# Another emission order for a fused linear-attention and gated feed-forward kernel

## The chip, the cores and the metric

The kernel runs on one core of one Trainium2 chip. The metric is the device time of one execution in microseconds (us), the median of several runs. The core has five engines with a queue each, which take their own instructions strictly in the order in which the program emitted them: TensorE (PE in the profile, its weight loads PEld), VectorE (DVE), ScalarE (ACT), GpSimd (POOL) and SyncE (SP, which here only issues transfers). Sixteen DMA engines move data between the chip's memory and the on-chip memory; they are fed by the queue of SP (q1 in the profile) and that of POOL (q0).

## The reference

```python
# attention, for each batch b of 4, head h of 8, step t of 768; head size 48
cur = einsum('bhd,bhe->bhde', u * k_t, v_t)
y_t = einsum('bhd,bhde->bhe', r_t, state + cur)
state = w_t[..., None] * state + einsum('bhd,bhe->bhde', k_t, v_t)
# feed-forward on x = y as (3072 tokens, 384)
xn  = x / sqrt(mean(x * x) + 1e-6) * rms_g
g   = xn @ w_gate                      # 384 x 1536
out = (g * sigmoid(g) * (xn @ w_val)) @ w_out
```

Inputs and output are float32; the kernel's matrix products run in bf16.

## The kernel before, in words

The 768 steps are cut into six **stages** n = 0 to 5 of 128 steps; each stage holds the four batches j = 0 to 3, so 512 tokens. Work is written as small named steps `name.n.j`; in the feed-forward steps the third number f = 0 to 11 is a block of 128 of the 1536 hidden units. One text, `ORDER` (line 25 on), lists all 1106 steps; the loop at the end of the kernel calls them one by one, and each call emits its instructions. So the order on every engine, in the load queue of SP and in the queue of POOL is written out by hand: a step that waits holds up all later steps of its engine. `ORDER` also sets which PSUM bank a step gets: `psum` takes, from a ring of two banks ("a" and "b") or four ("q"), a free one whose last use is oldest, so a matrix product may also have to wait for the last reader of what was in its bank.

One stage and batch of the attention, in the order of its data, with the lines of the profile in brackets:

- `load_r`, `load_k`, `load_v` (L244): 192 KB each on SP's queue. `load_w` (L257): 384 KB for stages 0 and 1 together, later 192 KB.
- `ln`, then `cs_mm` on PE (L391 to L409), the running sum of logarithms; `exp_r`, `exp_k` on ACT (L231); from stage 2 on `cs_add` on DVE (L417) between them.
- `r_mul` on DVE (L440), `k_mul` on DVE in stage 0 and on POOL later (L446), `w_tot` (L436).
- `rk_pe` on PE (L469) and `rk_tr` on ACT (L478) transpose the two in stages 0 and 1; from stage 2 on `rk_tr` is a transposing transfer on SP (L474).
- `q_mm` (L487, L489) multiplies them, and `q_mask_e` (DVE, L494), `q_copy_o` (ACT, L498) and `q_mask_o` (POOL, L505; in stage 0 DVE, L502) mask the result.
- `cast_v` (ACT, L374, in stages 0 and 1; POOL, L376, later), `st_mm` (L515) and `st_new` (DVE, L521 and L522) carry the state from stage to stage.
- `bonus_mul` (two POOL instructions, L452 and L453), `bonus_sum` (DVE, L457) and `bonus_v` (POOL, L462) make the term with u.
- `y_mm` (L535), `x_add` (DVE, L540); `x_sq` (ACT, L545), `x_rstd` (ACT in stage 0, POOL later, L553 and L554), `xn_mul` (ACT, L558); `xn_pe` (L569) and `xn_out` (DVE, L580) transpose the normalized rows into `xnt` in stages 0 to 3; in stages 4 and 5 `xn_tr` and `xn_gain` do so with transfers.

The feed-forward of a stage needs `xnt` of all four batches: `gate_mm` and `val_mm` (both L598, three matrix products 128x512 each), `silu` on ACT (L231) and `h_mul` on DVE (L616), for twelve f, then `o_mm` (L630, twelve products), `o_out` and `out_dma` (L645) for four batches. `gate_mm` uses ring "a", `val_mm` ring "b". While PE does the feed-forward of stage n, the attention of stage n + 1 is worked in between, and `o_mm` of a stage fills the time at the next boundary between stages.

Weights come over POOL's own DMA queue: `load_gv` (L346) brings w_gate (tile `wg_sb`) and w_val (tile `wv_sb`). `load_gv.0.1` and `load_gv.0.0` are w_val and w_gate for f = 0 to 3 (384 KB each in bf16), `load_gv.1.0` and `load_gv.1.1` are w_gate and w_val for f = 4 to 11 (768 KB each). `load_wo` brings w_out in three parts. They stand in POOL's queue, so each is issued when POOL reaches it.

Finally 48 steps `warm` (L369) are single matrix products on zeros; nobody reads them, and they keep PE at work while it has nothing else to do.

What holds the buffers: eight each of `rt`, `kt`, `vt`, three of `ruk`, six of `ydiag` and `rkT`.

Of the kernel before, what the change touches and what calls it, by code (L numbers as in the profile page):

```python
# [55 lines left out]
xn_mul.1.0 bonus_v.1.3 x_add.1.3 cs_mm.2.0 cs_add.2.0 st_new.1.2 x_sq.1.3 o_mm.0.0 o_out.0.0 out_dma.0.0 load_v.2.2
exp_r.2.0 w_tot.2.0 r_mul.2.0 w_tot.2.1 r_mul.2.1 o_mm.0.1 xn_pe.1.0 load_k.2.3 xn_out.1.0 exp_k.2.1 ln.2.2 cs_mm.2.2
cs_add.2.2 x_rstd.1.1 x_rstd.1.2 st_mm.1.3 st_new.1.3 xn_mul.1.2 xn_pe.1.2 xn_out.1.2 ln.2.3 cs_mm.2.3 o_mm.0.2
x_rstd.1.3 o_out.0.1 xn_mul.1.3 xn_pe.1.3 exp_k.2.0 xn_mul.1.1 xn_pe.1.1 exp_r.2.2 bonus_mul.2.1 k_mul.2.1 load_k.2.2
rk_tr.2.1 k_mul.2.0 rk_tr.2.0 bonus_mul.2.0 cast_v.2.1 o_mm.0.3 cs_add.2.3 exp_k.2.3 k_mul.2.3 xn_out.1.1 xn_out.1.3  # L60
load_v.2.0 w_tot.2.2 load_v.3.2 load_v.3.0 load_v.2.3 r_mul.2.2 bonus_mul.2.3 cast_v.2.2 exp_k.2.2 k_mul.2.2 rk_tr.2.2
exp_r.2.3 r_mul.2.3 rk_tr.2.3 load_w.3.0 load_k.3.1 w_tot.2.3 cast_v.2.0 o_out.0.2 gate_mm.1.7 silu.1.7 bonus_sum.2.1
bonus_v.2.1 bonus_sum.2.0 gate_mm.1.1 silu.1.1 val_mm.1.1 h_mul.1.1 val_mm.1.0 gate_mm.1.6 silu.1.6 val_mm.1.6
h_mul.1.6 load_r.3.1 out_dma.0.1 load_w.3.2 load_w.3.1 st_mm.2.1 st_new.2.1 gate_mm.1.0 gate_mm.1.5 silu.1.0 h_mul.1.0
load_r.3.2 o_out.0.3 out_dma.0.3 load_k.3.0 silu.1.5 val_mm.1.5 h_mul.1.5 gate_mm.1.4 silu.1.4 q_mm.2.0 q_mask_e.2.1
q_copy_o.2.0 q_mask_o.2.0 bonus_sum.2.3 q_mask_e.2.0 q_copy_o.2.1 q_mask_o.2.1 val_mm.1.7 h_mul.1.7 gate_mm.1.8
silu.1.8 st_mm.2.0 st_mm.2.2 gate_mm.1.9 st_new.2.2 load_w.3.3 bonus_v.2.0 bonus_v.2.3 bonus_mul.2.2 st_new.2.0
y_mm.2.1 gate_mm.1.3 silu.1.3 val_mm.1.3 h_mul.1.3 y_mm.2.0 gate_mm.1.2 load_r.3.0 load_r.3.3 x_add.2.0 val_mm.1.2
silu.1.2 h_mul.1.2 x_sq.2.0 silu.1.9 cast_v.2.3 cast_v.3.0 x_rstd.2.0 val_mm.1.4 h_mul.1.4 gate_mm.1.10 silu.1.10
x_add.2.1 x_sq.2.1 load_k.3.2 val_mm.1.9 h_mul.1.9 q_mm.2.2 q_mask_e.2.3 q_copy_o.2.2 load_k.3.3 out_dma.0.2  # L70
# [612 lines left out]
```

## Time and profile before

| what | value |
|---|---|
| runs shown | 203.05, 203.21 and 203.41 us, median 203.21 us |
| profiled execution, first to last instruction (span) | 202.2 us |
| median of the runs less that span | 1.0 us |
| instructions | 4444 |
| mean granted TensorE clock | 0.999 |
| busy: DVE, ACT, POOL | 146.1, 136.6, 134.3 us |
| bytes read from the chip's memory, written | 25.96 MB, 4.72 MB |
| first product of the feed-forward (`val_mm.0.2`) | 33.19 us after the span's start |
| last product of the kernel (`o_mm.5.4`) ends | 199.3 us |

The page lists each engine's busy time, the span in 40 slices of about 5.06 us with a busy digit in tenths for each, the DMA queues, the chain of work that ended last, and groups of instructions by line. Busy time of PE is modelled, since matrix products are pipelined: two that follow each other overlap in the list by about 0.2 us, so starts are compared here rather than ends. A time such as "33.19" is counted from the start of the span. The execution's own time is known as its span; what lies around it is taken as the 1.0 us of the table.

### The profile page before, as it was taken

What the parts mean: (1) busy time and instruction counts of PE and PEld (TensorE: products, weight loads), DVE (VectorE), ACT (ScalarE), POOL (GpSimd) and SP (SyncE); (2) the same over time, 40 slices, a digit from 0 to 9 for tenths busy, and PEclk for the clock granted to TensorE, in tenths of its full rate; (3) what the DMA queues carried; (4) which work ended last, traced back from release to release, by engine and by line L of the source; (5) the groups of instructions that cost most, each with busy time, mean ns of one, the idle gap of its engine ahead of it and who ended that gap; (6) DMA issues with size and microseconds to landing.
All of it is one profiled execution on the core that took longest, in us unless ns stands there. A gap on an engine that the chain in (4) does not pass through costs nothing.

```text
span 202.2 us, 4444 instructions
## 1 busy us (share of the span) xinstructions
PE 192.6 (95%) x1600; PEld 113.5 (56%) x1600; DVE 146.1 (72%) x289; ACT 136.6 (68%) x278; POOL 134.3 (66%) x198
## 2 busy tenths in 40 slices
PE   1999988899999999999999999999999999999994
...
GB/s 152 243 244 177 209 182 202 202 161 201 199 192 221 196 179 238 225 133 194 177 231 245 206 171 195 216 241 134 24 192 112 15 68 71 45 3 117 0 97 99
DMA packets 121566, 32.41 MB, mean 160 GB/s; under 512 B 116420, under 2 KB 120392, under 8 KB 121544
## 3 DMA queue, kind: packets, MB, share of 16 engines
...
HBM read 25.96 MB, written 4.72 MB: 152 GB/s over the span
## 4 chain that ended last, share of the span: by engine, by line
PE 79%; SPq 8%; DMA 8%; POOL 2%; issue 1%; ACT 0%; POOLq 0%
PE ps_av L598 12%; PE ps_bu L598 12%; PE ps_bv L598 10%; PE ps_au L598 10%; PE ps_qx L630 8%; PE ps_qv L630 7%; SPq L244 7%; DMA wg_sb<-in_moe_w_gate_dram 6%; PE ps_qz L630 5%; PE ps_qu L630 3%; SPq L257 2%; DMA kt<-in_k_dram 2%; PE ps_qu L487 1%; PE ps_av L406 1%; PE ps_qu L515 1%
## 5 line engine op out<-in xcount | busy, mean ns | idle before, releaser
L630 PEld LDWEIGHTS <-ht 128*128 128x128 bf16 x300 | 28.3, 98 | 16.9
L231 ACT ACTIVATE sg<-ps_av 128x512 bf16<-128x512 f32 x38 | 22.7, 598 | 18.4 <-PE ps_av L598 16.8
L616 DVE TENSOR_TENSOR ht<-ps_bu,sg 128x512 bf16<-128x512 f32 x38 | 26.1, 686 | 11.7 <-PE ps_bu L598 8.4
L598 PEld LDWEIGHTS <-wg_sb 128*128 128x128 bf16 x216 | 22.8, 114 | 20.2 <-DMA wg_sb<-in_moe_w_gate_dram 2.1
L598 PEld LDWEIGHTS <-wv_sb 128*128 128x128 bf16 x216 | 23.2, 114 | 19.3 <-DVE xnt L580 0.2
L616 DVE TENSOR_TENSOR ht<-ps_bv,sg 128x512 bf16<-128x512 f32 x34 | 23.3, 686 | 12.2 <-PE ps_bv L598 8.8
L452 POOL TENSOR_TENSOR ruk<-rt,kt 128x384 f32<-128x384 f32 x24 | 24.0, 1000 | 11.1 <-DMA kt<-in_k_dram 6.0
L598 PE MATMUL ps_av<-xnt,wg_sb 128*128 128x512 bf16 x114 | 30.9, 380 | 0.4 <-DMA wg_sb<-in_moe_w_gate_dram 0.4
L231 ACT ACTIVATE sg<-ps_au 128x512 bf16<-128x512 f32 x34 | 20.4, 599 | 16.0 <-PE ps_au L598 14.6
L598 PE MATMUL ps_bu<-xnt,wv_sb 128*128 128x512 bf16 x114 | 30.9, 380 | 0.0
L598 PE MATMUL ps_au<-xnt,wg_sb 128*128 128x512 bf16 x102 | 27.7, 381 | 0.8 <-DMA wg_sb<-in_moe_w_gate_dram 0.8
L598 PE MATMUL ps_bv<-xnt,wv_sb 128*128 128x512 bf16 x102 | 27.7, 380 | 0.0
L453 POOL TENSOR_TENSOR ruk<-ruk,u_bc 128x384 f32<-128x384 f32 x24 | 23.9, 997 | 1.9
L462 POOL TENSOR_TENSOR ydiag<-vt,diag 128x384 f32<-128x384 f32 x24 | 19.7, 830 | 0.9 <-DVE diag L457 0.8
L446 POOL TENSOR_TENSOR rk<-kt,ek 128x384 bf16<-128x384 f32 x20 | 19.9, 1003 | 0.3 <-ACT ek L231 0.3
L505 POOL TENSOR_SCALAR_AFFINE_SELECT qts<-qts 128x512 bf16<-128x512 bf16 x20 | 12.5, 636 | 10.7 <-ACT qts L498 10.7
L630 PE MATMUL ps_qx<-wo_sb,ht 128*128 128x384 bf16 x96 | 16.9, 326 | 0.0
L630 PE MATMUL ps_qv<-wo_sb,ht 128*128 128x384 bf16 (+1 forms) x96 | 15.9, 316 | 0.0
L558 ACT ACTIVATE xn<-xb,rstd 128x384 bf16<-128x384 f32 x24 | 14.1, 608 | 1.2 <-POOL rstd L554 1.2
L457 DVE TENSOR_REDUCE diag<-ruk 128x8 f32<-128x384 f32 x24 | 12.9, 543 | 2.7 <-POOL ruk L453 2.7
L231 ACT ACTIVATE lw<-wt 128x384 bf16<-128x384 f32 (+1 forms) x20 | 11.2, 579 | 4.6 <-DMA wt<-in_w_dram 4.5
L229 ACT ACT_TABLE_LOAD x10 | 12.8, 1283 | 1.8 <-PEq L667 1.6
...
## 6 DMA issues: line engine op xcount, KB each, us to landing
...
wg_sb<-in_moe_w_gate_dram POOLq DMA_DIRECT2D x1, 768.0 KB, 12.0
```

Of the source, the lines that this page charges most:

```text
L229: nc.scalar.preload_act_table_set(table_name)
L231: return nc.scalar.activation(**kw).ins
L244: dmas["load_" + which, n, j] = nc.sync.dma_start(out=inp[which, n, j], in_=t[j, :, n * L:(n + 1) * L, :].rearrange("h t d -> t h d")).ins
L446: eng.tensor_tensor(out=rk[:, n % 2, j, 1, :, 0:D], in0=inp["k", n, j], in1=bank["cs_k", n, j][:, 0:DM].rearrange("p (h d) -> p h d", h=H) ...
L452: nc.gpsimd.tensor_tensor(out=ruk[n, j], in0=inp["r", n, j], in1=inp["k", n, j], op=ALU.mult)
L453: nc.gpsimd.tensor_tensor(out=ruk[n, j], in0=ruk[n, j], in1=u_bc, op=ALU.mult)
L457: nc.vector.tensor_reduce(out=diag[n, j].rearrange("p h o -> p (h o)"), in_=ruk[n, j], axis=mybir.AxisListType.X, op=ALU.add)
L462: nc.gpsimd.tensor_tensor(out=ydiag[n, j], in0=inp["v", n, j], in1=diag[n, j].to_broadcast([128, H, D]), op=ALU.mult)
L558: nc.scalar.activation(out=xn, in_=xb[n, j], func=AF.Copy, scale=rstd[n, j][:, 1:2])
L598: nc.tensor.matmul(ps, lhsT=units(ws, c, f), rhs=xnt[n][:, c, :], start=(c == 0), stop=(c == KC - 1))
L616: nc.vector.tensor_tensor(out=ht[n][:, f, :], in0=bank.pop(("v", n, f)), in1=bank.pop(("sg", n, f)), op=ALU.mult)
L630: nc.tensor.matmul(ps[:, cols], lhsT=ht[n][:, f, b * L:(b + 1) * L], rhs=wo_sb[:, f, cols], start=(f == 0), stop=(f == FC - 1))
```

## The change

The list of steps is the same, step for step; its order is another one on every engine, in SP's load queue and in POOL's queue. With the order the choice of PSUM banks changes too, by the rule above. Two constants are written in another way: `EXPK_SB` still holds the same pairs, since `K_POOL` has 10 to 13 as well, and `GV_BEHIND` has a third `None`, which nothing reads.

What can be seen when the order is read engine by engine: on PE, 43 of the 48 `warm` steps stand ahead of the first `cs_mm`, and all 48 ahead of the first `rk_pe` (before: 5 ahead of the first `cs_mm`, and the rest spread up to the start of the feed-forward). In SP's queue the first twenty loads are in another order. In POOL's queue `load_gv.0.1`, `load_gv.0.0` and `load_gv.1.0` follow each other with nothing between them, and `load_gv.1.1` comes six steps of attention later. From stage 1 on most steps of the attention stand somewhat earlier among the products of the feed-forward. The start of the list, and the lines further down that the prediction speaks of:

```diff
-load_r.0.1 load_w.0.1 load_k.0.0 load_k.0.1 ln.0.1 warm.31.0 load_w.0.0 ln.0.0 warm.0.0 warm.13.0 warm.28.0
-bonus_mul.0.1 bonus_sum.0.1 load_r.0.0 load_v.0.0 bonus_mul.0.0 load_w.0.2 load_w.0.3 warm.29.0 load_k.0.2 load_v.0.1
-load_r.0.2 bonus_mul.0.2 load_r.0.3 load_v.0.3 load_v.0.2 bonus_v.0.1 load_r.1.3 load_k.1.0 cs_mm.0.1 exp_k.0.1
-warm.10.0 warm.17.0 warm.33.0 warm.38.0 exp_r.0.1 r_mul.0.1 k_mul.0.1 bonus_sum.0.0 bonus_v.0.0 cs_mm.0.0 exp_r.0.0
-ln.0.2 exp_k.0.0 cast_v.0.0 r_mul.0.0 k_mul.0.0 w_tot.0.0 warm.8.0 warm.16.0 warm.12.0 warm.4.0 warm.30.0 w_tot.0.1
-rk_pe.0.1 warm.15.0 warm.14.0 load_k.0.3 bonus_mul.0.3 load_r.1.1 load_r.1.0 load_k.1.1 load_v.1.1 load_r.1.2 ln.0.3
-load_k.1.3 warm.20.0 warm.37.0 warm.2.0 warm.22.0 warm.23.0 warm.5.0 warm.3.0 rk_pe.0.0 warm.24.0 load_gv.0.1
-load_k.1.2 load_v.1.0 load_w.2.1 warm.25.0 load_v.1.2 load_w.2.0 load_v.1.3 load_r.2.1 load_r.2.0 load_w.2.2 warm.32.0
-warm.27.0 st_mm.0.0 st_new.0.0 load_w.2.3 cs_mm.0.2 rk_tr.0.1 q_mm.0.1 warm.19.0 rk_tr.0.0 exp_r.0.2 cast_v.0.1
-r_mul.0.2 warm.7.0 cs_mm.0.3 q_mask_e.0.1 q_mm.0.0 warm.6.0 warm.18.0 warm.11.0 warm.26.0 warm.1.0 warm.21.0 warm.36.0
-exp_k.0.2 w_tot.0.2 k_mul.0.2 rk_pe.0.2 q_mask_e.0.0 bonus_sum.0.2 bonus_v.0.2 exp_r.0.3 w_tot.0.3 q_mask_o.0.0
-r_mul.0.3 warm.39.0 y_mm.0.0 warm.9.0 cs_mm.1.0 cast_v.0.3 q_mask_o.0.1 x_add.0.0 load_k.2.1 load_gv.0.0 cast_v.0.2
-exp_k.0.3 k_mul.0.3 rk_tr.0.2 q_mm.0.2 q_mask_o.0.2 q_mask_e.0.2 y_mm.0.1 x_add.0.1 exp_r.1.0 bonus_sum.0.3 r_mul.1.0
-rk_pe.0.3 cs_mm.1.1 x_sq.0.0 warm.34.0 x_rstd.0.0 rk_tr.0.3 q_mm.0.3 q_mask_o.0.3 exp_r.1.1 exp_k.1.0 exp_k.1.1
-warm.40.0 warm.35.0 x_sq.0.1 x_rstd.0.1 xn_mul.0.0 xn_mul.0.1 y_mm.0.2 q_mask_e.0.3 warm.44.0 warm.42.0 x_add.0.2
-warm.41.0 st_mm.0.3 st_new.0.3 warm.43.0 x_sq.0.2 x_rstd.0.2 w_tot.1.1 w_tot.1.0 bonus_v.0.3 y_mm.0.3 x_add.0.3
-x_sq.0.3 xn_mul.0.2 x_rstd.0.3 xn_pe.0.0 xn_out.0.0 st_mm.0.2 xn_pe.0.1 cs_mm.1.3 exp_r.1.3 st_new.0.2 xn_out.0.1
-r_mul.1.1 load_gv.1.0 k_mul.1.0 st_mm.0.1 warm.47.0 rk_pe.1.0 warm.45.0 st_new.0.1 xn_pe.0.2 xn_out.0.2 cs_mm.1.2
-xn_mul.0.3 exp_k.1.3 xn_pe.0.3 r_mul.1.3 xn_out.0.3 cast_v.1.1 k_mul.1.1 load_gv.1.1 rk_pe.1.1 st_mm.1.1 exp_k.1.2
-exp_r.1.2 w_tot.1.2 r_mul.1.2 w_tot.1.3 bonus_mul.1.3 val_mm.0.2 val_mm.0.3 warm.46.0 gate_mm.0.2 gate_mm.0.3 rk_tr.1.1
-q_mm.1.1 silu.0.2 h_mul.0.2 load_k.2.0 silu.0.3 h_mul.0.3 bonus_sum.1.3 st_new.1.1 gate_mm.0.0 val_mm.0.1 rk_tr.1.0
-bonus_mul.1.0 val_mm.0.0 load_r.2.3 silu.0.0 q_mask_e.1.1 h_mul.0.0 bonus_mul.1.1 bonus_sum.1.1 gate_mm.0.6 silu.0.6
-gate_mm.0.1 silu.0.1 q_mm.1.0 q_copy_o.1.0 gate_mm.0.5 silu.0.5 h_mul.0.1 q_mask_e.1.0 bonus_sum.1.0 gate_mm.0.7
-silu.0.7 load_r.2.2 k_mul.1.3 rk_pe.1.3 q_mask_o.1.0 gate_mm.0.9 k_mul.1.2 rk_pe.1.2 q_copy_o.1.1 rk_tr.1.2 gate_mm.0.4
-cast_v.1.0 load_wo.0.0 val_mm.0.6 h_mul.0.6 val_mm.0.5 h_mul.0.5 y_mm.1.0 bonus_v.1.1 bonus_v.1.0 x_add.1.0 load_v.2.1
-st_mm.1.0 st_new.1.0 rk_tr.1.3 silu.0.9 val_mm.0.4 val_mm.0.7 silu.0.4 h_mul.0.4 h_mul.0.7 x_sq.1.0 cast_v.1.2
...
+load_k.0.0 load_r.0.0 load_w.0.0 load_v.0.1 load_w.0.2 load_w.0.1 load_v.0.0 bonus_mul.0.0 warm.24.0 load_r.0.1
+warm.10.0 warm.22.0 warm.29.0 warm.17.0 warm.4.0 warm.43.0 warm.26.0 ln.0.1 cast_v.0.1 ln.0.2 ln.0.0 cast_v.0.0
+warm.39.0 warm.31.0 warm.19.0 load_w.0.3 warm.18.0 load_k.0.1 bonus_sum.0.0 bonus_v.0.0 bonus_mul.0.1 warm.32.0
+warm.16.0 bonus_sum.0.1 warm.33.0 warm.14.0 warm.40.0 warm.42.0 warm.8.0 warm.5.0 warm.27.0 load_k.0.2 warm.28.0
+warm.2.0 warm.11.0 warm.3.0 warm.30.0 warm.37.0 load_r.0.2 load_v.1.1 bonus_mul.0.2 warm.23.0 warm.41.0 load_k.0.3
+warm.1.0 warm.34.0 warm.36.0 warm.20.0 warm.7.0 load_k.1.0 load_r.0.3 warm.0.0 warm.35.0 warm.13.0 warm.25.0 warm.9.0
+ln.0.3 warm.38.0 warm.12.0 warm.6.0 warm.15.0 cs_mm.0.1 exp_r.0.1 warm.21.0 warm.45.0 cs_mm.0.0 r_mul.0.1 exp_k.0.1
+k_mul.0.1 warm.47.0 warm.46.0 warm.44.0 load_r.1.1 load_v.0.3 w_tot.0.1 exp_k.0.0 exp_r.0.0 rk_pe.0.1 load_v.0.2
+k_mul.0.0 rk_tr.0.1 r_mul.0.0 st_mm.0.0 w_tot.0.0 st_new.0.0 rk_pe.0.0 rk_tr.0.0 bonus_sum.0.2 q_mm.0.1 q_mask_e.0.1
+q_mask_o.0.1 cs_mm.0.2 cast_v.1.1 bonus_mul.0.3 bonus_v.0.1 exp_k.0.2 exp_r.0.2 q_mm.0.0 q_mask_e.0.0 k_mul.0.2
+cs_mm.0.3 cast_v.0.3 r_mul.0.2 y_mm.0.1 q_mask_o.0.0 rk_pe.0.2 exp_k.0.3 y_mm.0.0 k_mul.0.3 cast_v.0.2 exp_r.0.3
+w_tot.0.2 rk_tr.0.2 x_add.0.0 bonus_v.0.2 load_gv.0.1 st_mm.0.3 load_r.1.0 load_k.1.1 load_k.1.2 w_tot.0.3 r_mul.0.3
+cs_mm.1.0 load_gv.0.0 load_gv.1.0 bonus_mul.1.0 q_mm.0.2 load_r.1.3 load_r.1.2 load_k.1.3 x_add.0.1 cs_mm.1.1
+q_mask_o.0.2 q_mask_e.0.2 x_sq.0.0 x_rstd.0.0 st_new.0.3 rk_pe.0.3 exp_k.1.0 xn_mul.0.0 st_mm.0.1 y_mm.0.2 exp_r.1.1
+rk_tr.0.3 xn_pe.0.0 load_v.1.0 w_tot.1.1 x_add.0.2 r_mul.1.1 load_v.1.2 load_v.1.3 bonus_sum.0.3 q_mm.0.3 exp_k.1.1
+x_sq.0.1 cs_mm.1.3 q_mask_e.0.3 q_mask_o.0.3 exp_r.1.0 k_mul.1.1 bonus_v.0.3 k_mul.1.0 rk_pe.1.1 y_mm.0.3 x_rstd.0.1
+x_sq.0.2 xn_out.0.0 w_tot.1.0 x_add.0.3 r_mul.1.0 xn_mul.0.1 st_mm.0.2 load_w.2.1 load_w.2.0 x_rstd.0.2 st_mm.1.1
+x_sq.0.3 xn_mul.0.2 x_rstd.0.3 xn_mul.0.3 cs_mm.1.2 st_new.0.1 st_new.0.2 xn_pe.0.2 xn_pe.0.1 xn_out.0.2 xn_out.0.1
+exp_r.1.3 bonus_mul.1.3 xn_pe.0.3 rk_pe.1.0 exp_k.1.3 k_mul.1.3 load_gv.1.1 exp_k.1.2 xn_out.0.3 bonus_sum.1.0
+bonus_mul.1.1 rk_tr.1.1 exp_r.1.2 val_mm.0.3 r_mul.1.3 w_tot.1.3 w_tot.1.2 r_mul.1.2 val_mm.0.2 q_mm.1.1 gate_mm.0.2
+gate_mm.0.3 silu.0.2 bonus_v.1.0 load_w.2.3 load_w.2.2 load_r.2.1 k_mul.1.2 q_mask_e.1.1 silu.0.3 st_new.1.1 rk_pe.1.3
+gate_mm.0.0 h_mul.0.3 h_mul.0.2 bonus_sum.1.1 rk_tr.1.0 gate_mm.0.1 q_mm.1.0 q_copy_o.1.1 cast_v.1.0 val_mm.0.1
+st_mm.1.0 val_mm.0.0 silu.0.0 silu.0.1 q_copy_o.1.0 gate_mm.0.6 q_mask_o.1.0 h_mul.0.0 q_mask_e.1.0 h_mul.0.1 silu.0.6
+rk_pe.1.2 gate_mm.0.5 st_new.1.0 gate_mm.0.7 silu.0.5 bonus_v.1.1 load_wo.2.0 load_r.2.0 y_mm.1.0 silu.0.7 rk_tr.1.3
+gate_mm.0.9 gate_mm.0.4 x_add.1.0 load_wo.0.0 bonus_mul.1.2 bonus_sum.1.3 val_mm.0.6 q_mm.1.3 h_mul.0.6 bonus_sum.1.2
+rk_tr.1.2 val_mm.0.5 q_mm.1.2 x_sq.1.0 cast_v.1.2 q_copy_o.1.3 val_mm.0.4 h_mul.0.5 q_mask_e.1.2 st_mm.1.2 val_mm.0.7
+x_rstd.1.0 q_mask_o.1.1 bonus_v.1.3 silu.0.4 load_wo.1.0 silu.0.9 h_mul.0.4 q_mask_e.1.3 h_mul.0.7 q_mask_o.1.3
...
+x_add.1.2 st_mm.1.3 val_mm.0.8 val_mm.0.10 x_add.1.3 x_add.1.1 xn_out.1.0 load_k.2.1 h_mul.0.8 ln.2.0 cs_mm.2.1
...
+o_mm.0.3 w_tot.2.2 k_mul.2.0 rk_tr.2.0 r_mul.2.3 w_tot.2.3 load_v.2.0 r_mul.2.2 st_new.2.1 bonus_mul.2.0 gate_mm.1.7
+val_mm.1.1 load_k.2.2 silu.1.7 k_mul.2.3 bonus_mul.2.3 cast_v.2.0 load_v.2.2 gate_mm.1.1 val_mm.1.0 gate_mm.1.6
+k_mul.2.2 silu.1.1 silu.1.6 o_out.0.3 gate_mm.1.0 h_mul.1.1 bonus_sum.2.0 bonus_sum.2.1 silu.1.0 cast_v.2.2 val_mm.1.6
...
+q_mask_o.2.0 q_mask_o.2.1 load_r.3.1 load_k.3.1 st_mm.2.0 gate_mm.1.4 st_mm.2.2 h_mul.1.5 rk_tr.2.3 load_v.2.3
...
+q_mask_o.3.2 q_copy_o.3.3 load_w.4.0 q_mask_o.3.3 x_add.3.1 silu.2.8 h_mul.2.3 y_mm.3.2 st_mm.3.3 bonus_v.3.2 x_sq.3.1
+x_rstd.3.1 load_r.4.1 load_w.4.2 load_r.4.3 x_add.3.2 silu.2.9 y_mm.3.3 x_sq.3.2 x_rstd.3.2 cast_v.4.0 xn_pe.3.0
...
+bonus_mul.4.1 bonus_mul.4.3 o_mm.2.1 cs_mm.4.0 load_v.4.2 out_dma.1.3 st_new.3.3 cs_add.4.0 exp_r.4.0 ln.4.2 cs_mm.4.1
...
+load_w.5.1 o_mm.2.2 cs_mm.4.2 load_v.5.1 out_dma.2.1 w_tot.4.1 r_mul.4.1 xn_out.3.3 cs_add.4.2 k_mul.4.0 k_mul.4.1
+o_mm.2.0 cs_mm.4.3 st_mm.4.0 o_out.2.2 exp_r.4.2 xn_out.3.1 cs_add.4.3 r_mul.4.2 bonus_sum.4.3 exp_k.4.3 exp_r.4.3
...
+x_sq.4.2 xn_tr.4.3 load_k.5.1 cs_mm.5.0 xn_tr.4.1 bonus_mul.5.3 cs_add.5.0 cs_mm.5.1 cs_add.5.1 exp_r.5.0 o_mm.3.1
+xn_gain.4.0 x_rstd.4.2 r_mul.5.0 cs_mm.5.3 exp_k.5.0 exp_r.5.1 xn_mul.4.2 bonus_sum.5.3 o_mm.3.2 st_new.4.2 k_mul.5.0
...
-    EXPK_SB = sel("10 11 12 13") | K_POOL
+    EXPK_SB = sel("") | K_POOL
...
-    GV_BEHIND = (None, None)
+    GV_BEHIND = (None, None, None)
```

142 lines of the change are left out of this document (65 added, 77 removed).

## The prediction, as it was put on record

> **What bounds the kernel now.** I read the page first: busy times, slices, chain.
>
> ```profile
> PE 192.6 (95%) x1600; PEld 113.5 (56%) x1600; DVE 146.1 (72%) x289; ACT 136.6 (68%) x278; POOL 134.3 (66%) x198
> ...
> PE   1999988899999999999999999999999999999994
> ...
> PE 79%; SPq 8%; DMA 8%; POOL 2%; issue 1%; ACT 0%; POOLq 0%
> ```
>
> PE is the bound, and the chain is PE from about 40 us on. Next the table of windows, for the rest of the run:
>
> ```profile
> 45.00:199.30 154.30, 154.29 (x1239) 91.25 (x1237) 116.72 (x222) 104.78 (x215) 105.42 (x155) 1.00 0.71 150
> ```
>
> PE (second number) fills 154.29 of 154.30 us. An order can win nothing there but the few tenths at which products start late. The waits of PE, and its timeline around the handoff to the feed-forward:
>
> ```profile
> PE ps_qu L328 <- POOL ones_row L324: 4.1, 1, 4.1
> PE ps_au L598 <- DMA wg_sb<-in_moe_w_gate_dram: 0.8, 1, 0.8
> PE ps_qu L535 <- DVE qts L502: 0.6, 1, 0.6
> PE ps_av L598 <- DMA wg_sb<-in_moe_w_gate_dram: 0.4, 1, 0.4
> ```
>
> ```profile
> 33.19 0.81 PE L598 MATMUL ps_bu<-xnt,wv_sb 128*128 128x512 bf16 x3
> ...
> 34.48 0.33 PE L369 MATMUL ps_qz<-zero 128*128 128x384 bf16 x1
> 35.64 0.84 PE L598 MATMUL ps_au<-xnt,wg_sb 128*128 128x512 bf16 x3 [0.83 <-DMA wg_sb<-in_moe_w_gate_dram]
> ...
> 39.90 0.84 PE L598 MATMUL ps_av<-xnt,wg_sb 128*128 128x512 bf16 x3 [0.38 <-DMA wg_sb<-in_moe_w_gate_dram]
> ```
>
> So two val_mm start at 33.19, but the first gate_mm waits for w_gate until 35.64, and gate_mm.0.6 for its second part until 39.90. Where those transfers come from, in POOL's timeline (L346 issues them):
>
> ```profile
> 22.47 1.00 POOL L452 TENSOR_TENSOR ruk<-rt,kt 128x384 f32<-128x384 f32 x1 [3.39 <-DMA kt<-in_k_dram]
> ...
> 24.49 0.99 POOL L346 DMA_DIRECT2D wv_sb<-in_moe_w_val_dram  x1
> ...
> 26.29 0.81 POOL L346 DMA_DIRECT2D wg_sb<-in_moe_w_gate_dram  x1
> ...
> 27.90 0.80 POOL L346 DMA_DIRECT2D wg_sb<-in_moe_w_gate_dram  x1
> ```
>
> They stand behind the last bonus_mul of stage 0, which waits for k(0,3). Time is decided by **when the feed-forward starts and what PE loses after that**.
>
> **The yardstick.** PE's work left after a step is the sum of starts to starts: 0.648 us a gate_mm or val_mm, 1.948 an o_mm, 0.553 a paired q_mm, 0.446 an rk_pe, 0.374 a y_mm, 0.17 an st_mm or xn_pe, 0.27 a cs_mm. After gate_mm.0.2 that is 161.3 us in the old order, 161.0 in the new one (q_mm.1.1 is done by then). Start plus work left: before, 35.64 + 161.3 = 196.9; the last product ended at 199.3, so 2.4 us were lost later: 0.55 at gate_mm.0.6, 0.15 at val_mm.1.8, 1.7 in tenths at changes of shape, which I carry over.
>
> **The start, walked through.** Loads: the first 22 landings of before, by bytes ahead of them, give the clock of SP's queue (4,224 KB at 22.40, 4,416 KB at 23.20). In the new order r(0,3) is item 16 (3,840 KB, 20.4), v(0,3) 18 (22.4), v(0,2) 19 (23.2); before, k(0,3) was last at 22.4.
>
> Warm products: PE starts them at 5.94 as before, 0.32 each until the clock rises at about 11.1 (16 of them), then 0.163: 43 end at 15.5. Only then comes cs_mm.0.1, 8 us later than before (7.51). ACT then has all of stage 0 ahead of it: 8 exponentials and 4 of stage 1 at 0.40, 4 rk_tr at 0.89, 3 casts at 0.40, x_sq, x_rstd and xn_mul at 0.50, 0.44 and 0.50 for four batches, 16 us in all. It is caught by loads twice, at cast_v.0.3 and cast_v.0.2 (23.25), and from there runs without a gap to xn_mul.0.3 (32.84 to 33.4). xn_pe and xn_out add 1.0: **val_mm at 34.4 instead of 33.19**. ACT, not the load of weights, is late here.
>
> POOL: bonus_v.0.2 waits for v(0,2) and ends at 24.15; then the three transfers follow at once, 24.15, 25.15, 25.95 instead of 24.49, 26.29, 27.90. Queue q0 is at work without a break either way, so I move its landings by the first start alone, 0.3 us: w_gate at 35.3 (before 35.59) and 39.5. PE: two val_mm, q_mm.1.1 (rk_tr.1.1 ends at 35.5), gate_mm.0.2 at 36.06: 36.06 + 161.0 = 197.0, level with before. But now PE has rk_pe.1.3, q_mm.1.0 and st_mm.1.0 to do before gate_mm.0.6, which comes at 41.0, after the weights; 41.0 + 156.1 = 197.1, where before had 39.90 + 157.7 = 197.6. **So far -0.5 us.**
>
> **What takes it back.** (a) v(1,0), 26th in both load queues. The timeline of SP and the view of that tile:
>
> ```profile
> 25.64 1.30 SPq L244 DMA_DIRECT2D vt<-in_v_dram  x1
> ...
> 30.66 6.49 SPq L244 DMA_DIRECT2D vt<-in_v_dram  x1
> ```
>
> ```profile
> DMA to landing us min/median/max: 2.8/3.7/15.1
> ```
>
> The load issued at 25.64 took 15.1 us, because from 32 to 40 us, with q0 on 2,048-byte pieces, q1 moved 17 KB/us instead of 200 (packet records). Before, nothing waited for it until 45.6 (cast_v.1.0 on ACT). In the new order ACT reaches that cast at 39.45, ahead of silu.0.0, and POOL reaches bonus_v.1.0 at 38. If it lands at 40.7 again, silu.0.0 and with it gate_mm.0.6 slip by 1.1; if load_gv.1.1, issued 4 to 5 us later than before (30.63), leaves q1 room from 37 on, by nothing. I take 0.4. (b) w_val for f over 3: needed at 45.05 (before 45.16); landed 44.16, and now is issued at 35.2 into a queue that has hardly run dry: 0 to 1, taken 0.2. (c) Leads that the new order makes shorter than any that sufficed before: st_mm.4.0 5.1 us after its cs_mm (8.7), cs_mm.5.3 2.3 after the reader of its bank was fed (4.3), cs_mm.4.2 2.6, xn_pe.3.0 1.3, st_mm.1.3 1.3, and st_mm.2.2, whose k(2,2) now stands behind rk_tr.2.0 on SP: 0 to 0.5 each, 0.6 in all. The boundaries themselves have the old lead or more (last y_mm to first product of stage 3: 14.6 instead of 7.8 us). SP and POOL work past stage 2 I cost at nothing, since PE's feed-forward covers it: q_mm needs its rk_tr 10 us after cs_mm at the least in both orders, the transfer itself taking 3.4; a queue that is later than that lead stops PE for the excess. The tail, o_mm.5.4 to the last store, and the ten table loads are the same. EXPK_SB and GV_BEHIND: nothing.
>
> Sum: -0.5 + 0.4 + 0.2 + 0.6 = **+0.7 us**: a span of 202.9 against 202.2, and with the 1.0 us around it 203.9 against the median of 203.21.
>
> **A rule against it.** The rows: from 34 to 40 us q0 and q1 moved nearly the same number of packets in each 2 us (189 and 187, 193 and 195, 183 and 180). The Trainium skill, "DMA: Bandwidth & Descriptors", section "Queues, rings and completion order", says that each DMA engine goes round its queues packet by packet; the trace agrees. By it, three weight transfers back to back bring no byte sooner and only lengthen the loads beside them, which is my rival 2.
>
> **Rivals.**
> 1. *The weights decide and nothing new stalls: faster.* Place: gate_mm.0.2. Around 18.5 to 19.5 q1 moved only 67 KB/us; without such a dip v(0,2) lands 0.8 us sooner, and ACT's run, POOL's transfers and w_gate (34.5) all move with it. Decides from v(0,2) before 22.8 on. It gives -0.5 to -1.3: 202.3. For: the long leads. Against: ACT's 16 us.
> 2. *Starved loads: slower.* k(1,3) is item 25, at 5,568 KB; q1 had moved 5,669 KB by 32.0, when the large pieces begin. If it is 100 KB short, it lands near 37; bonus_mul and k_mul (3.1 us) hold rk_pe.1.3 until 40.2 (+2.8), and load_gv.1.1 behind them lands some 9 us later, 1 us too late: 206.5.
> 3. *PE bound, nothing to measure:* +0.7 is inside what my 0 to 0.5 terms can lose: 203.2.
> 4. *The clock:* all warm products now end by 18 us, and PE has gaps up to 0.8 us until 34. If the clock fell back once, 5.1 us at 0.32 instead of 0.163 cost 2.6 us: 206. Against it, gaps of 0.8 did nothing before.
>
> **Numbers.** Chances: the forecast (203.9) 0.36, rival 1 0.33, rival 3 0.13, rival 2 0.15, rival 4 0.03. Faster by over 0.2% (what a measurement here can tell, 0.4 us): 0.33; same 0.13; slower 0.54. The range takes in the ends of the unknown costs: below, rival 1's -1.3 and 0.4 of the 1.7 us of tenths, 201.5; above, rival 2 with 0.5 more for (c), 207.0.
>
> **What would show it.** First val_mm at 34.4, gate_mm.0.2 at 36.1 with no DMA wait; cs_mm.0.1 at 15.5; L346 at 24.2, 25.2, 26.0 and 35; ACT waiting for vt near 40; PE nearly full from 45 on. Wrong if POOL waits for kt at 31 to 37, if PE shows gaps over 1 us after 45, or if w_gate lands well before 35.

## The result, and the profile after

| | before | after |
|---|---|---|
| median of four runs (lowest, highest), us | 203.13 (202.83, 203.41) | 210.19 (209.49, 211.87) |
| profiled execution: span, us | 202.2 | 207.8 |
| first `val_mm`, us | 33.19 | 34.47 |
| `gate_mm.0.2`, us | 35.64 | 36.19 |
| `gate_mm.0.6`, us | 39.90 | 45.85 |
| PE busy from 45.00 to 199.30, us | 154.29 | 152.74 |

The changed kernel is slower: ratio 1.0348, 95% interval 1.0295 to 1.0402. The forecast was 203.9, the range 201.5 to 207.0; the time lies above both, and 3.7 us above the 206.5 of rival 2 (starved loads). In every run that lists both numbers, time less span is 1.66 to 1.77 us, so the span that belongs to before's median is 201.4: the profiled execution of before was 0.8 us longer than usual, the one of after 0.7 us shorter. In two of the experiments the profiled execution is one of a few that took longer than the rest of the same kernel and are left out of its ratio; those profiles are read for the mechanism alone.

Lines after L327 have moved down by one against before (`load_gv` L347, `bonus_mul` L453, `k_mul` L447, `rk_pe` L470, `gate_mm` and `val_mm` L599). The page of after, busy times, slices and chain:

```profile
PE 193.2 (93%) x1580; PEld 114.6 (55%) x1600; DVE 145.9 (70%) x289; ACT 136.8 (66%) x278; POOL 134.6 (65%) x198
...
PE   1999878499999999999999999999999999999994
...
PEclk9999999979999999999999999999999999999999
...
PE 63%; SPq 16%; DMA 11%; POOL 7%; issue 2%; ACT 0%; POOLq 0%
```

The same amount of PE work takes a longer span. One slice, the eighth, has a 4, and the slice behind it a lower clock; the chain spends 27% on SP's queue and DMA, where before had 16%. PE's timeline at that slice:

```profile
34.47 0.81 PE L599 MATMUL ps_bu<-xnt,wv_sb 128*128 128x512 bf16 x2
...
36.19 0.84 PE L599 MATMUL ps_av<-xnt,wg_sb 128*128 128x512 bf16 x3
36.87 0.81 PE L599 MATMUL ps_au<-xnt,wg_sb 128*128 128x512 bf16 x3
37.52 0.39 PE L470 MATMUL ps_qz<-ident,rk 128*128 128x128 bf16 x4
40.93 0.61 PE L470 MATMUL ps_qz<-ident,rk 128*128 128x128 bf16 x4 [3.02 <-POOL rk L447]
41.33 1.49 PE L599 MATMUL ps_av<-xnt,wg_sb 128*128 128x512 bf16 x3
42.61 1.49 PE L599 MATMUL ps_au<-xnt,wg_sb 128*128 128x512 bf16 x3
```

The feed-forward starts as predicted and no product waits for a weight. Then PE stands in the middle of `rk_pe.1.3` for `k_mul.1.3`, and the two `gate_mm` behind the gap take 1.49 us where others take 0.81. POOL's timeline has the cause:

```profile
23.68 0.98 POOL L347 DMA_DIRECT2D wv_sb<-in_moe_w_val_dram  x1
24.68 1.56 POOL L347 DMA_DIRECT2D wg_sb<-in_moe_w_gate_dram  x2
...
30.31 1.00 POOL L447 TENSOR_TENSOR rk<-kt,ek 128x384 bf16<-128x384 f32 x1
37.85 0.99 POOL L453 TENSOR_TENSOR ruk<-rt,kt 128x384 f32<-128x384 f32 x1 [6.54 <-DMA kt<-in_k_dram]
...
39.88 0.99 POOL L447 TENSOR_TENSOR rk<-kt,ek 128x384 bf16<-128x384 f32 x1
40.81 0.80 POOL L347 DMA_DIRECT2D wv_sb<-in_moe_w_val_dram  x1
```

POOL waits 6.54 us for k(1,3), issued at 24.74 as the 25th load; `bonus_mul`, `k_mul` and the last weight transfer stand behind it. In before the same load was the 24th and landed at 27.9, and the same `bonus_mul` started without a wait:

```profile
31.45 1.01 POOL L452 TENSOR_TENSOR ruk<-rt,kt 128x384 f32<-128x384 f32 x1
```

The DMA view of two neighbouring stretches of 2 us in after, 24 to 26 and 26 to 28 (packets, MB, share of the 16 engines), shows why it came so late:

```profile
q1 hardware_dynamic: 2155, 0.41, 100.7%
q0 software_dynamic: 22, 0.02, 17.7%
```

```profile
q0 software_dynamic: 241, 0.25, 84.4%
q1 hardware_dynamic: 204, 0.04, 17.2%
```

While q0 has work, the two queues move about as many packets each, and q1's are 192 bytes against 1,024: 19 KB/us instead of 198. This happens with the 1,024-byte pieces of the first transfers, not only with the 2,048-byte pieces from 32 us on; q1 gets room only where q0 falls off for a moment (404 packets against 43 in the half microsecond from 28.5). The Trainium skill, "DMA: Bandwidth & Descriptors", section "Queues, rings and completion order", has each DMA engine go round its queues packet by packet; these counts agree, if a packet of the profile is one of the page's.

The table of windows there (us, busy time of PE, PEld, DVE, ACT, POOL, then the granted clock), first one row of before, then two of after:

```profile
40.00:45.00 5.00, 5.00 (x42) 2.91 (x43) 3.41 (x7) 3.63 (x7) 2.41 (x4) 1.00 0.90 172
```

```profile
35.00:40.00 5.00, 2.90 (x22) 1.38 (x21) 3.87 (x9) 4.95 (x8) 2.07 (x3) 1.00 1.01 196
40.00:45.00 5.00, 4.07 (x21) 1.75 (x22) 0.55 (x1) 1.58 (x4) 4.90 (x6) 0.66 1.08 183
```

The account of the 5.6 us between the two profiled spans, from start to start of PE's steps against the durations of the prediction's yardstick: `gate_mm.0.2` starts 0.55 us later with 0.3 us less work left; `rk_pe.1.3` loses 3.4 us, in before nothing; the lower clock adds 1.3 us at `gate_mm.0.0` and `gate_mm.0.1`; the weight wait of `gate_mm.0.6` and small ones are gone (-0.7); and from 45 us on another 1.3 us are lost in places of 0.1 to 0.4 us. The sum is 5.55 us. The medians differ by 7.06 us; the other 1.5 us are the 0.8 and 0.7 by which the two profiled executions differ from the usual ones, and no trace shows where those lie.

### The profile page after: what moved, and what is told of

Same layout as the page of the kernel before. It is cut to its first block, busy times and chain, and to the rows that moved or that the text cites. A ratio compares the mean times of both kernels' runs of the same rounds, so it can differ in the third digit from the quotient of the medians.

```text
span 207.8 us, 4419 instructions
## 1 busy us (share of the span) xinstructions
PE 193.2 (93%) x1580; PEld 114.6 (55%) x1600; DVE 145.9 (70%) x289; ACT 136.8 (66%) x278; POOL 134.6 (65%) x198
## 4 chain that ended last, share of the span: by engine, by line
PE 63%; SPq 16%; DMA 11%; POOL 7%; issue 2%; ACT 0%; POOLq 0%
SPq L245 12%; PE ps_av L599 10%; PE ps_bu L599 9%; PE ps_bv L599 9%; PE ps_au L599 8%; PE ps_qv L631 7%; DMA kt<-in_k_dram 6%; PE ps_qz L631 5%; PE ps_qx L631 4%; PE ps_qu L631 4%; SPq L258 3%; DMA rkT<-rk 2%; POOL rk L447 2%; DMA rt<-in_r_dram 2%; POOL ruk L454 1%
## 5 line engine op out<-in xcount | busy, mean ns | idle before, releaser
L232 ACT ACTIVATE sg<-ps_av 128x512 bf16<-128x512 f32 x37 | 22.1, 597 | 21.6 <-PE ps_av L599 20.7
L617 DVE TENSOR_TENSOR ht<-ps_bv,sg 128x512 bf16<-128x512 f32 x37 | 25.4, 687 | 12.8 <-PE ps_bv L599 6.8
L599 PEld LDWEIGHTS <-wg_sb 128*128 128x128 bf16 x216 | 23.4, 115 | 19.6 <-issue 1.1
L599 PEld LDWEIGHTS <-wv_sb 128*128 128x128 bf16 x216 | 23.0, 114 | 18.7 <-issue 0.3
L617 DVE TENSOR_TENSOR ht<-ps_bu,sg 128x512 bf16<-128x512 f32 x35 | 24.0, 687 | 12.5 <-PE ps_bu L599 8.7
L453 POOL TENSOR_TENSOR ruk<-rt,kt 128x384 f32<-128x384 f32 x24 | 24.0, 1002 | 11.9 <-DMA kt<-in_k_dram 8.9
L599 PE MATMUL ps_av<-xnt,wg_sb 128*128 128x512 bf16 x109 | 30.7, 387 | 0.2
L232 ACT ACTIVATE sg<-ps_au 128x512 bf16<-128x512 f32 x35 | 20.9, 598 | 12.8 <-PE ps_au L599 12.0
L599 PE MATMUL ps_bv<-xnt,wv_sb 128*128 128x512 bf16 x103 | 28.8, 380 | 0.3
L599 PE MATMUL ps_au<-xnt,wg_sb 128*128 128x512 bf16 x99 | 28.5, 388 | 0.3
L599 PE MATMUL ps_bu<-xnt,wv_sb 128*128 128x512 bf16 x101 | 28.3, 380 | 0.2
L447 POOL TENSOR_TENSOR rk<-kt,ek 128x384 bf16<-128x384 f32 x20 | 19.8, 1001 | 1.0 <-ACT ek L232 1.0
L631 PE MATMUL ps_qv<-wo_sb,ht 128*128 128x384 bf16 x84 | 14.8, 326 | 0.0
L546 ACT ACTIVATE junk<-xb 128x384 bf16<-128x384 f32 x24 | 12.5, 520 | 1.9 <-DVE xb L541 1.7
```

Of the source, the lines that this page charges most:

```text
L232: return nc.scalar.activation(**kw).ins
L447: eng.tensor_tensor(out=rk[:, n % 2, j, 1, :, 0:D], in0=inp["k", n, j], in1=bank["cs_k", n, j][:, 0:DM].rearrange("p (h d) -> p h d", h=H) ...
L453: nc.gpsimd.tensor_tensor(out=ruk[n, j], in0=inp["r", n, j], in1=inp["k", n, j], op=ALU.mult)
L599: nc.tensor.matmul(ps, lhsT=units(ws, c, f), rhs=xnt[n][:, c, :], start=(c == 0), stop=(c == KC - 1))
L617: nc.vector.tensor_tensor(out=ht[n][:, f, :], in0=bank.pop(("v", n, f)), in1=bank.pop(("sg", n, f)), op=ALU.mult)
L631: nc.tensor.matmul(ps[:, cols], lhsT=ht[n][:, f, b * L:(b + 1) * L], rhs=wo_sb[:, f, cols], start=(f == 0), stop=(f == FC - 1))
```

## The experiments

Each ratio is to the kernel before on the same chip. All edits are moves in `ORDER`; lines of "..." leave out the steps between.

**Load k(1,3) earlier in the new order: a_k13_early.** The theory is rival 2; its own rival is that something else in the new order costs the time.

```diff
 load_k.1.1
-load_k.1.2
+load_k.1.3
...
 load_r.1.2
-load_k.1.3
+load_k.1.2
```

> The new order with one edit in the load queue: load_k.1.3 (25th) and load_k.1.2 (22nd) change places. Theory A (place of one load): the early loss, 3.5 us of waiting at rk_pe.1.3 and the half clock behind it, comes from k(1,3) alone; now bonus_mul.1.3 starts without a wait near 31.3, rk_pe.1.3 by 37.4, load_gv.1.1 is issued near 34.5, and the time is 204.5 to 205.5, some 5 us under the 210.2 of the new order. Theory B (weights back to back): whatever load stands 25th is starved, so the loss only moves to k(1,2), whose k_mul.1.2 then holds POOL ahead of q_mask_o.1.0: 207 or more.

Measured: 205.07 us (203.96 to 206.71), ratio 1.013 (1.0056 to 1.0204). k(1,3) landed at 25.0 us, POOL's list of waits has no entry for `kt`, so the loss did not move to k(1,2) as theory B has it, and PE goes from `gate_mm.0.3` through `rk_pe.1.3` (36.94) to `gate_mm.0.0` (37.38). The window from 40 to 45 us:

```profile
40.00:45.00 5.00, 5.00 (x43) 3.02 (x41) 3.84 (x7) 4.01 (x8) 3.92 (x7) 1.00 1.04 193
```

PE is full and the clock 1.00. Of the 7.1 us, 2.7 stay here, and 3.2 when the same kernel ran on another chip (a_k13_again, below): two loads exchanged take back 3.8 to 4.4 us. So the wait for k(1,3), with what stands behind it, was the main cause, and 1.3 to 1.8% have another.

**Use rk_pe.1.3 later: a_rkpe13_late.** `rk_pe.1.3` moves from behind `gate_mm.0.3` to just ahead of `rk_tr.1.3`, behind `gate_mm.0.7`, as before had it; the load stays 25th.

```diff
-rk_pe.1.3
 gate_mm.0.0
...
 silu.0.7
+rk_pe.1.3
 rk_tr.1.3
```

> The new order with rk_pe.1.3 moved on PE from behind gate_mm.0.3 to behind gate_mm.0.7 (loads and POOL as they were). Theory A: k(1,3) still lands near 37.8; PE goes on with gate_mm.0.0 at 37.9 and doesn't lose 3.5 us there nor the clock, but load_gv.1.1 stands behind k_mul.1.3 on POOL and lands near 49.8, so val_mm.0.6 waits for w_val from about 46: 208 to 209. If PE's own place in the queue were the whole cause: 205.

Measured: 206.62 us (206.18, 207.07), ratio 1.020 (1.0141 to 1.0258), between the two. k(1,3) landed at 35.3 in this execution, POOL waited 3.88 us, and PE lost 0.7 us at `rk_pe.1.2` and 0.5 ahead of `val_mm.0.6` (w_val, landed 47.15) in place of 3.4 at `rk_pe.1.3`; the clock stayed at 1.00. The late load is not harmless with `rk_pe.1.3` at its old place. How much the early place adds is not shown: there are two executions, and in the profiled one the load landed 2.5 us earlier than in after.

**Keep PE at work during the wait: a_warm_in_wait.** 20 more `warm` products ahead of `rk_pe.1.3`.

> The new order with twenty more products on zeros (0.163 us each, 3.3 us in all) ahead of rk_pe.1.3, so that PE is at work while it waits; nothing that is needed gets longer, if k(1,3) lands near 37.8 as before. If the half clock after the wait (granted 0.66 from 40 to 45 us) has a price of its own, it goes: the granted clock stays at 1.0 and the time is 1.3 to 1.6 us lower, 208.7. If the clock falls only because of the wait and costs nothing beside it, the time is 210.2 again.

Measured: 209.34 us (209.28, 209.40), ratio 1.0333 (1.0279 to 1.0387). It tells little: k(1,3) landed at 33.6 this time, before the added products (38.0 to 42.0) were through, so they took the place of the wait instead of filling it. The clock stayed at 1.00, and `gate_mm.0.0` and `gate_mm.0.1` lost 0.1 us together instead of 1.4, which fits a price of about 1.3 us for the clock.

**Space the weight transfers: a_gv_spaced.** `load_gv.0.0` behind `bonus_mul.1.0`, `load_gv.1.0` behind `k_mul.1.1`; the load stays 25th.

```diff
 load_gv.0.1
-load_gv.0.0
-load_gv.1.0
 bonus_mul.1.0
+load_gv.0.0
...
 k_mul.1.1
+load_gv.1.0
```

> The new order with POOL work put between the weight transfers again: load_gv.0.0 behind bonus_mul.1.0, load_gv.1.0 behind k_mul.1.1 (issued near 25.9 and 27.8, about as in the kernel before). Theories A and B both: q1 keeps 60 to 80 KB/us until about 32, k(1,3) lands by 32 and the wait at rk_pe.1.3 goes; the price is that gate_mm.0.2 waits for w_gate until near 35.6 and gate_mm.0.6 hardly: 204.5 to 205.5. If k(1,3) still lands after 36, the spacing isn't what starves it, but the start of the first transfer at 23.7: 209 to 210.

Measured: 205.77 us (205.29, 206.25), ratio 1.0157 (1.0098 to 1.0217); `bonus_mul.1.3` started at 32.1 without a wait. Between 28 and 30 us, while q0 had little, q1 moved 341 KB (after: 165). So it is q0's unbroken work that starves the load, as expected, though the time is 0.3 us above the expected range. The first part of w_gate, issued 2.0 us later than in after, landed only 0.5 us later (33.7), so that "back to back" had brought little; `gate_mm.0.2` came at 36.94 and not at 35.6, but behind a first `val_mm` at 35.22, not behind a weight.

**The late place alone, in the old order: b_k13_late.**

```diff
-load_k.1.3
+load_k.1.2
...
-load_k.1.2
+load_k.1.3
```

> The kernel before with load_k.1.3 and load_k.1.2 exchanged in the load queue, so that k(1,3) is the 25th load there too, while the weight transfers keep their old places (first bytes on q0 at 26.9 us in the profile of before). Theory A (the later place harms only because the weights begin about 0.9 us earlier in the new order): q1 passes 5,568 KB near 30.5 us, k(1,3) lands at 31 to 32, bonus_mul.1.3 starts within 1 us of 31.45, rk_pe.1.3 (42.8) has room, and the time is that of before: ratio 0.998 to 1.003. Theory B (the 25th place alone starves it): k(1,3) lands near 37, rk_pe.1.3 goes some 2 us late and the ratio is 1.008 to 1.015.

Measured: ratio 1.0014 (0.9986 to 1.0042), the time of theory A; but of ten executions two took 210.3 us and one 205.6, which this ratio leaves out. Only one of the two longest was profiled, so no trace shows the load in time. In that one q1 had moved only 5,152 KB when q0 began at 27.0:

```profile
41.86 0.98 POOL L453 TENSOR_TENSOR ruk<-rt,kt 128x384 f32<-128x384 f32 x1 [10.68 <-DMA kt<-in_k_dram]
```

```profile
PE ps_qv L488 <- DVE st L523: 5.2, 1, 5.2
```

A place as late as that is a question of which execution one gets. Over eight profiles, in KB from the packet records (q0 begins where about ten of its packets are through):

| kernel | k(1,3) ends at | q0 begins, us | q1 by then | short by | landed or used, us |
|---|---|---|---|---|---|
| before | 5,376 | 26.9 | 5,359 | 17 | 27.9 |
| a_warm_in_wait | 5,568 | 26.4 | 5,368 | 200 | 33.6 |
| a_gv_spaced | 5,568 | 26.3 | 5,356 | 212 | 32.1 |
| a_rkpe13_late | 5,568 | 26.1 | 5,324 | 244 | 35.3 |
| after | 5,568 | 26.0 | 5,183 | 385 | 37.8 |
| b_gv_early | 5,376 | 26.4 | 5,171 | 205 | 37.5 |
| b_k13_late | 5,568 | 27.0 | 5,152 | 416 | 41.8 |
| a_k13_early | 4,992 | 26.1 | 5,327 | none | 25.0 |

With the first two weight transfers issued 1.0 to 1.8 us apart, a load that is 200 KB or more short when q0 begins comes 7 to 15 us after that moment; with 3.05 us between them, in a_gv_spaced, within 6. At 26 us q1 had moved between 4,852 and 5,319 KB in the fifteen profiles, and between 5,084 and 5,319 in the six that have k(1,3) as the 22nd load, so the outcome varies by more than 100 KB either way.

**Weights earlier in the old order: b_gv_early.**

```diff
 load_gv.0.1
+load_gv.0.0
...
 bonus_v.0.2
-load_gv.0.0
```

> The kernel before with load_gv.0.0 moved directly behind load_gv.0.1, ahead of bonus_v.0.2: the first part of w_gate is issued 0.8 us earlier, bonus_v.0.2 0.8 us later (x_add.0.2 starts 1.1 us after it ended, so that it has room). If the start of w_gate's transfer sets gate_mm.0.2, that product starts 0.5 to 0.8 us sooner and the ratio is 0.996 to 0.998. If q0 only shares its bytes between two transfers, w_val lands later and w_gate at nearly the old time: 0.999 to 1.001. If k(1,2), the 25th load, is starved and holds POOL, the ratio is over 1.003.

Measured: 203.71 us (201.93 to 206.13), ratio 1.0020 (0.9991 to 1.0049). The ratio lies between the second and the third case. In the profiled execution, the longest of twelve, `gate_mm.0.2` came at 34.4, and a load was starved, though not the one expected: k(1,3), here the 24th, landed at 37.5. PE's waits there and the window from 40 to 45 us:

```profile
PE ps_qv L488 <- DVE st L523: 1.6, 1, 1.6
PE ps_qz L470 <- POOL rk L447: 1.3, 1, 1.3
```

```profile
40.00:45.00 5.00, 2.32 (x23) 1.42 (x23) 3.72 (x8) 1.62 (x4) 4.84 (x6) 1.00 1.02 200
```

In this execution the starved load takes more than the earlier weights give. The clock stays at 1.00 here with several waits of up to 1.6 us, while one of 3.0 us lowered it in after.

**The use of k(1,3) later, with it: b_k13_use_late.** On top of b_gv_early, `bonus_mul.1.3` goes behind `bonus_mul.1.1` and `bonus_sum.1.3` behind `bonus_sum.1.1`.

> The kernel of b_gv_early (the order before, load_gv.0.0 directly behind load_gv.0.1) with the use of k(1,3) moved instead of its load: bonus_mul.1.3 behind bonus_mul.1.1 on POOL, bonus_sum.1.3 behind bonus_sum.1.1 on DVE. In b_gv_early gate_mm.0.2 came at 34.2 us, and k(1,3), landing at 37.5, then cost 3.9 us between q_mm.1.0 and rk_pe.1.2. If the late load costs only through what is queued behind its first use, POOL does the products of batches 0 and 1 meanwhile, the losses at q_mm.1.0, rk_pe.1.3 and rk_pe.1.2 fall below 1 us together and the ratio to the order before is 0.990 to 0.998. If the load must itself be early, it stays at 1.000 to 1.004.

Measured: 203.44 us (202.25 to 205.48) against 203.63, ratio 0.9983 (0.996 to 1.0007): not to be told from no change. In the profiled execution k(1,3) landed at 31.9, early enough, so it doesn't show the case that it was made for. No version here beats the kernel before.

**What is left in the new order.** The first theory was the one late transpose that a_k13_early shows, 1.02 us at `q_mm.4.2`: a_q42_late moves that step behind `gate_mm.3.9`.

> The new order with k(1,3) exchanged with k(1,2) in the load queue (as in a_k13_early: span 203.4 us, ratio 1.013) and q_mm.4.2 moved behind gate_mm.3.9, two products later. In a_k13_early q_mm.4.2 stood 1.02 us in the middle of its products for rkT(4,3), whose transpose was issued behind load_w.5.2 on SP and landed 4.3 us after it. Two products cover 1.1 us. If that wait is a real part of what is left: 0.4 to 1.0 us less than a_k13_early, ratio 1.008 to 1.011. If PE loses the time in another place instead: ratio 1.013 again.

Measured: 207.81 us (207.0 to 208.51), ratio 1.0241 (1.0212 to 1.0271): a miss. PE lost 0.3 us ahead of `q_mm.4.2` and 0.8 at `st_mm.4.2` instead, and 0.7 each behind `cs_mm.4.1` and `cs_mm.4.3`.

For the start, a_warm_spread moves 27 of the 43 `warm` products behind `cs_mm.0.1`, `cs_mm.0.0` and `rk_pe.0.0`.

> The new order with k(1,3) exchanged with k(1,2) (as in a_k13_early) and 27 of the 43 warm products ahead of cs_mm.0.1 moved behind it, nine each behind cs_mm.0.1, cs_mm.0.0 and rk_pe.0.0. Theory of the prediction (ACT's run from cast_v.0.2, which waits for v(0,2), sets the first val_mm; the warm products only delay work that has room): cs_mm.0.1 starts 3 to 6 us earlier, the first val_mm stays within 0.3 us of 33.9 and the ratio of a_k13_early, 1.013, stays. Rival (the warm products push ACT's run back): the first val_mm comes 0.5 to 1.5 us earlier and the ratio is 1.006 to 1.010.

Measured: 208.11 us (205.91 to 208.55), ratio 1.0236 (1.0192 to 1.0279), a miss for both. `cs_mm.0.1` came 3.2 us earlier, the first `val_mm` 2.4 us later: v(0,2) landed 1.1 us later than in a_k13_early, and `cs_mm.0.2` came at 21.6 instead of 19.1, so that ACT reached `cast_v.0.2` at 24.4. What the theory rested on held: from `cast_v.0.2` to the end of `xn_mul.0.3` ACT took 10.3 to 11.0 us in ten profiles of the new order. Taking the products off the front did not bring the feed-forward forward here; why `cs_mm.0.2` and v(0,2) came later is not shown.

Then SP's queue. In a_k13_early it issues from 64 to 120 us with no gap over 0.6 us; an extract of its timeline:

```profile
107.72 1.70 SPq L245 DMA_DIRECT2D kt<-in_k_dram  x2
109.47 0.78 SPq L258 DMA_DIRECT2D wt<-in_w_dram  x1
110.29 0.97 SPq L245 DMA_DIRECT2D rt<-in_r_dram  x1
```

w(4,0), r(4,1), w(4,2), r(4,3) land within 0.2 us of their use, while r(5,1), issued at 92.4, is used at 147.6. In before the tightest of the loads of stages 3 to 5 whose landing is on record came 1.3 us ahead of its use. a_k13_again is a_k13_early once more; a_sp_urgent moves four long-lead loads back:

```diff
-load_r.5.1
...
-load_v.4.3
-load_v.5.0
...
-load_r.5.3
...
 load_w.4.3
+load_r.5.1 load_v.4.3 load_v.5.0 load_r.5.3
```

> The kernel of a_k13_early once more (new order, k(1,3) exchanged with k(1,2)), to stand beside the next run on the same chip. a_k13_early gave a ratio of 1.013, two kernels built on it 1.024; with loads that land at the moment of their use its time should spread: ratio 1.010 to 1.025.

> a_k13_again with four loads that have 25 to 52 us to their use, load_r.5.1, load_v.4.3, load_v.5.0 and load_r.5.3, moved behind load_w.4.3 in SP's queue. In a_k13_early SP issued without a gap from 64 to 120 us, and w(4,0), r(4,1), w(4,2), r(4,3), w(4,3) and k(4,0) landed within 0.2 us of their first use; the four issues ahead of them took 0.7 to 1.2 us each. Theory A (SP's issues are late in stages 3 and 4 and cost what is lost at cs_mm.4.0 to 4.3 and q_mm.4.2, 0.9 to 2.4 us in four profiles): these loads land 2 to 3 us ahead of their use, the losses between 112 and 123 us fall below 0.3 us and the run is 0.6 to 1.5 us below a_k13_again. Theory B (DVE, ACT or POOL are late there by their own order): no difference over 0.3 us.

Measured: 206.87 us, ratio 1.0181 (1.0126 to 1.0236), and 207.78 us, ratio 1.0212 (1.0157 to 1.0266). In the profile of a_k13_again `gate_mm.0.2` starts 0.9 us later than in before, and from there on PE loses 2.2 us more than in before. PE's waits from 112 to 140 us, first a_k13_again, then a_sp_urgent:

```profile
PE ps_qz L516 <- DVE xnt L581: 1.1, 1, 1.1
PE ps_qz L488 <- DMA rkT<-rk: 0.6, 1, 0.6
```

```profile
PE ps_qz L488 <- DMA rkT<-rk: 1.4, 1, 1.4
PE ps_qx L631 <- DVE ob L638: 0.7, 1, 0.7
```

The loads now landed 1.8 to 2.9 us ahead and the losses at `cs_mm.4.x` went, as theory A says; but the transposes and stores behind them came later, and PE lost the same again, 2.4 us, at `q_mm.4.2` and `o_mm.2.3`. So a_no_out01 takes work out of the queue: the eight stores of stages 0 and 1.

> The kernel of a_k13_early without the eight stores out_dma.0.0 to 1.3: the rows of stages 0 and 1 are not written, and SP has eight issues fewer (0.4 to 1.0 us each) by 117 us; nothing else is changed. In a_sp_urgent the losses moved from cs_mm.4.x (112 to 123 us) to o_mm.2.3 and q_mm.4.2 (121 to 136 us) when four loads were only moved back. Theory A (SP's issues are short as a whole in stages 2 to 4, and reordering only hands the lateness on): with some 6 us of issues gone, w(4,0) to k(4,0) land 2 us or more ahead of their use and rk_tr.4.3 too, the losses of PE between 93 and 140 us that are over 0.31 us each add up to less than 0.5 us (0.9 to 2.9 in five profiles), and the ratio is 1.003 to 1.010. Theory B (the lateness comes from DVE, ACT or POOL): the losses stay, ratio 1.013 to 1.024.

Measured: 205.17 us (204.78 to 206.06), ratio 1.0139 (1.0107 to 1.0170). PE's waits from 112 to 140 us:

```profile
PE ps_qz L487 <- DMA rkT<-rk: 0.7, 1, 0.7
```

The losses at `cs_mm.4.x` are gone, and PE takes 1.8 us less from `gate_mm.0.2` on than in a_k13_again. `q_mm.4.2` still loses 0.8 us (the transpose of rk(4,3) was issued 3.0 us long and landed 5.7 us after its start), the loads landed only 0.2 to 2.0 us ahead, and the ratio misses the expected 1.003 to 1.010; it is no lower than the 1.013 of a_k13_early. That SP's queue is short of issues fits these traces but is not shown: a_gv_spaced, with all its stores, has no loss over 0.2 us at `cs_mm.4.x` either.

**Only the load queue: b_spq_new.** The old order on the engines, SP's queue in the new one, up to a few transposes and stores of stages 3 to 5.

> The order before on every engine, with SP's queue in the new order (out_dma.2.3, rk_tr.4.2 and rk_tr.4.3 alone keep a place behind what they need). POOL's queue is as before, so that load_gv.0.1 follows bonus_mul.0.3, which no longer waits for k(0,3) (14th load instead of 18th, landed 17.6 us in the profile of after). Theory A (the load queue carries most of the loss): the weights are issued near 22 us, before q1 has moved 4,600 KB, so that r(1,2) and k(1,3), at 5,376 and 5,568 KB, land at 37 us or later, POOL's bonus_mul.1.3 waits over 5 us, and the ratio is 1.015 to 1.040. Theory B (the engines' order carries it: ACT's run, the early rk_pe.1.3): with rk_pe.1.3 back at its old place behind gate_mm.0.7 the late loads find room, and the ratio is 0.998 to 1.006.

Measured: 244.88 us, ratio 1.2067 (1.1987 to 1.2146), far outside both. PE stands several times for `q_mask_o` on POOL:

```profile
PE ps_qu L536 <- POOL qts L506: 9.4, 1, 9.4
PE ps_qv L536 <- POOL qts L506: 6.7, 1, 6.7
```

POOL itself waits 10.1 us for r(4,1) and 10.0 us for k(5,3), while its `bonus_mul.1.3` starts without a wait at 36.0. This run says nothing on how the loss divides between the queue and the engines, only how much rests on the two agreeing past stage 2.

## Why the prediction was wrong, step by step

- **The walk to gate_mm.0.2 held.** `cs_mm.0.1` 14.87 (15.5 forecast), first `val_mm` 34.47 (34.4), `gate_mm.0.2` 36.19 without a weight wait (36.1). ACT's run sets it, as said. The weights were issued at 23.7 to 25.5 and w_gate landed at 33.1, 2.5 us earlier than in before and not 0.3: moving q0's landings by its first start alone was wrong, but nothing hung on it. What it was compared with was a long execution: in b_k13_late, with the old order on the engines, `gate_mm.0.2` came at 35.03, not 35.64.
- **The step that failed is the bound of the starved loads.** The prediction set k(1,3)'s 5,568 KB against the 5,669 KB that q1 had moved "by 32.0, when the large pieces begin", saw 100 KB in hand, and gave the case 0.15 and nothing in the sum. The starving begins with q0's first piece, not with the large ones: before's own trace has q1 at 5,359 KB at 26.9, when q0 begins. A load that ends at 5,568 KB was 209 KB short there already, and 385 with the transfers 0.9 us earlier. Both signs that the prediction gives for this came: POOL waited for `kt` from 31 us on, and w_gate landed well before 35. The path of rival 2 was right and its price nearly so: `rk_pe.1.3` was forecast for 40.2, at 2.8 us, and its second half ran at 40.93, at 3.4; the last weights, forecast 1 us too late, landed at 49.79, just ahead of `val_mm.0.6` at 49.92.
- **Rival 4's clock came as a part of rival 2,** not by itself: 1.3 us (2.6 forecast), after a wait and not after the warm products. No term of rival 2 or of the range held it.
- **SP and POOL past stage 2, costed at nothing, were probably not nothing.** The prediction hid them behind ten us from `cs_mm` to `q_mm`; that covers `rk_tr`, but not the loads that stand ahead of the next stage's `cs_mm`. In after w(4,2), w(4,3), r(4,3) and r(4,1) landed 0.02 to 0.25 us ahead of their use. PE lost 1.3 us from 45 us on, of which 0.4 at `q_mm.4.2` is for a transpose of SP; in a_k13_again it lost 2.4 us at `cs_mm.4.1`, `cs_mm.4.3` and `q_mm.4.2`. How much of this is SP's stays open. Term (c), 0.6 us for short leads, named `st_mm.4.0` but another reason.
- **Terms (a) and (b) were small.** v(1,0) landed at 38.4, ahead of `cast_v.1.0` at 39.6: nothing instead of 0.4. PE did not wait for w_val in after (0.2 taken); a_rkpe13_late lost 0.5 there.
- **The 1.0 us around the span** is 1.7, since the prediction took it from different executions; the mistake hid that the profiled execution of before was 0.8 us above its median.

The walk's -0.5 us, rival 2's wait at its forecast price of 2.8, 1.3 for the clock and 1.3 from 45 us on give a span of 207.1 against 207.8 measured; 0.6 of the difference is the wait, which was longer.
